# Hashed attention feeding a gated MLP: pair loads moved into the first layers and behind marks, earlier preparation of pairs, a new start

## The chip, the core and the metric

One core of a Trainium2 chip. The metric is the device time of one execution in microseconds (us), median of several. The profile's span is mostly 1.7 to 2.5 us shorter than the time of the same execution (once 3.5), because the time also holds what lies around the program's own instructions. A run over 1.5% above the fastest of its kernel is slow; all ratios are of fast runs, and where a kernel had slow runs, the time given here is the median of its fast ones.

## The reference, cut to what matters

```python
q_bits = (einsum('bhsd,dk->bhsk', q, proj) > 0)     # 6 hash bits per token
k_bits = (einsum('bhsd,dk->bhsk', k, proj) > 0)
mask   = q_bucket[:, :, :, None] == k_bucket[:, :, None, :]
scores = where(mask, scale * q @ k.T, -1e9)
attn   = softmax(scores)                            # B, H, S, D = 4, 8, 768, 64
x      = (attn @ v) as [B*S, H*D]                   # 3072 x 512
h      = x @ w_in;  g = h * cos(h);  out = g @ w_out  # d_ff 2048
```

Four batches of eight heads. Two heads make a pair (16 pairs, numbered 0 to 15). A head is six units; a unit is one score (two matmuls), one exponential on ScalarE over 128x768 and one value step (six matmuls). There are 192 units, 0 to 191; unit u holds the exponential number u + 1.

## The kernel before

The mask comes for free: six hash bits, scaled, are appended as rows to Q and K, so that only equal buckets survive the exponential. Preparing a pair takes: a load (three DMAs of 384 KB), casts to fp16 on GpSimd, 32x32 block transposes on VectorE, the hash on TensorE, and the transposition of Q and K. From pair 5 on the transposition is a DMA, started by SyncE; it brings Q and K in one piece, and VectorE then copies K's rows to their own tile. The bit rows go in by four small DMAs.

```python
    def load(pr, eng):                       # three DMAs; nat has three buffers
        ...
            eng.dma_start(out=t_, in_=heads_ap(src, pr))
    def dma_transposes(pr, hh):              # SyncE's queue
        nc.sync.dma_start_transpose(out=qx(pr)[...], in_=n16_rows(pr)[...])
    def k_copy(pr, hh):                      # VectorE: waits for that DMA
        nc.vector.tensor_copy(out=kx(pr)[0:D, hh, :], in_=qx(pr)[D:P, hh, :])
    def norm(h):                             # VectorE: the division of a head (cut)
        ...                                  # dv, tot, rc, and last:
            nc.vector.tensor_tensor(out=dst, in0=tot[:, :, 0:D], in1=rc..., op=ALU.mult)   # xn
    def xtrans(b, ft):                       # SyncE's queue again
        nc.sync.dma_start_transpose(out=xT[(b, ft)], in_=xn[(b, ft)]...)
    ...
        for n in range(1, NP):
            s0 = 12 * (n - 1) - (0 if n < NEARLY else 4 if n == NEARLY else 6)
            ...
            elif NEARLY + 1 < n < NP - 1:
                at(s0 - 1, lambda n=n: load(n + 1, nc.gpsimd))
            ...
                at(s0, start)                # casts, block transposes, cast of V
                at(s0 + 2, hsh)              # two DMA transposes
                at(s0 + (5 if n == NEARLY else 3), hsh2)   # hash
                at(s0 + 7, kc)               # K copies, bit rows
```

The first layer of the MLP (L1) of a batch stands in one block, TensorE alone, after unit 55, 103 and 151; the second layer is spread over the units of the next batch. L1 reads `xT`, so it needs the last division of its batch. VectorE, GpSimd and SyncE take their work in program order, as their timelines below show.

The softmax here doesn't subtract the row's maximum and nothing guards it: scores larger than these inputs give would overflow.

## Time and profile before

| | before |
|---|---|
| time, median (range) | 310.13 us (309.94 to 310.41) |
| span of the profiled run | 308.4 us |
| first exponential starts | 9.26 |
| 56th starts (last ahead of the first L1) | 58.91 |
| 104th (last ahead of the second L1) | 125.04 |
| 192nd (the last) | 254.75 |

The page's part on the chain that ended last says which engine's work the end can be followed back through:

```profile
PE 89%; ACT 6%; DVE 3%; issue 1%; ACTq 0%; DVEq 0%
```

### The profile page before, as it was taken

How to read it: one execution, taken by the hardware profiler on the slowest of the kernel's cores; microseconds unless marked ns; L12 is line 12 of the kernel's file. 1: busy time of each engine (PE TensorE's matmuls, PEld its weight loads, DVE VectorE, ACT ScalarE, POOL GpSimd, SP SyncE). 2: the span in 40 equal slices, each digit the busy share in tenths (PEclk: the TensorE clock that was granted, in tenths of full speed). 3: DMA queues.
4: the chain of work that ended last, by engine and by line, in shares of the span. 5: the costliest groups of instructions: out<-in, count | busy, mean ns of one | idle time of the engine just before them, and what ended most of it. 6: DMA issues, size and time to landing. Idle time of an engine off the chain costs nothing.

```text
span 308.4 us, 7711 instructions
## 1 busy us (share of the span) xinstructions
PE 300.1 (97%) x3090; PEld 182.8 (59%) x3090; DVE 201.8 (65%) x434; ACT 234.3 (76%) x288; POOL 109.4 (35%) x180
## 2 busy tenths in 40 slices
PE   8899999899999999999999999999999999999995
PEld 3577677556566666555566666555566664565444
DVE  3665466877598988866777878766777343577211
ACT  3788999977899999766899999766899993577000
POOL 4898258378384684400064584100030000000000
PEclk9999999999999999999999999999999999999998
DMA  6969969289469856700169979200133223100121
GB/s 205 376 109 163 333 86 214 33 140 192 163 172 268 215 162 168 217 2 0 45 80 234 234 146 199 48 18 2 53 62 89 68 62 94 36 0 0 62 76 69
DMA packets 45332, 37.74 MB, mean 122 GB/s; under 512 B 32264, under 2 KB 39200, under 8 KB 45296
## 3 DMA queue, kind: packets, MB, share of 16 engines
q1 hardware_dynamic: 38080, 19.35, 28.9%
q0 software_dynamic: 6576, 17.17, 21.0%
q10 hardware_dynamic: 640, 0.72, 0.7%
q8 instruction: 24, 0.39, 0.5%
q14 instruction: 12, 0.10, 0.1%
HBM read 27.26 MB, written 6.29 MB: 109 GB/s over the span
## 4 chain that ended last, share of the span: by engine, by line
PE 89%; ACT 6%; DVE 3%; issue 1%; ACTq 0%; DVEq 0%
PE m_ps L370 26%; PE s_ps L320 18%; PE s_ps L252 18%; PE av_ps L278 10%; PE m_ps L320 6%; ACT pt L258 5%; PE m_ps L164 4%; PE av_ps L320 2%; PE s_ps L408 1%; PE m_ps L354 1%; PE m_ps L224 1%; DVE g L337 1%; DVE blkq L151 1%; ACT cos L332 1%; PE av_ps L164 1%
## 5 line engine op out<-in xcount | busy, mean ns | idle before, releaser
L258 ACT ACTIVATE pt<-s_ps,exp_bias 128x768 f16<-128x768 f32 x192 | 161.7, 899 | 11.1 <-PE s_ps L252 9.7
L370 PE MATMUL m_ps<-wout,g 128*128 128x512 f16 x368 | 105.6, 379 | 0.1
L252 PE MATMUL s_ps<-qx,kx 128*128 128x512 f16 (+1 forms) x384 | 93.8, 326 | 2.6 <-ACT pt L258 1.2
L278 PEld LDWEIGHTS <-pt 128*128 128x128 f16 x1152 | 58.7, 97 | 21.7
L320 PEld LDWEIGHTS <-win 128*128 128x128 f16 x512 | 50.0, 98 | 34.6 <-issue 0.2
L278 PE MATMUL av_ps<-vx,pt 128*128 128x65 f16 x1152 | 65.7, 193 | 0.0
L320 PE MATMUL s_ps<-xT,win 128*128 128x384 f16 x352 | 62.3, 326 | 0.1
L337 DVE TENSOR_TENSOR g<-s_ps,cos 128x768 f16<-128x768 f32 x44 | 42.1, 958 | 28.1 <-ACT cos L332 28.1
L332 ACT ACTIVATE cos<-s_ps,cos_bias 128x768 f16<-128x768 f32 x44 | 39.7, 901 | 26.8 <-PE s_ps L320 25.4
L252 PEld LDWEIGHTS <-kx 128*128 128x128 f16 x384 | 35.2, 97 | 31.1 <-issue 3.3
L138 POOL CAST vx<-natv 128x768 f16<-128x768 f32 x16 | 13.3, 829 | 92.8 <-PE av_ps L278 87.8
L370 PEld LDWEIGHTS <-g 128*128 128x128 f16 x368 | 31.2, 98 | 20.1 <-issue 3.3
L376 DVE COPY ob<-m_ps 128x512 f32<-128x512 f32 x23 | 15.8, 686 | 22.6 <-PE m_ps L370 22.6
L320 PE MATMUL m_ps<-xT,win 128*128 128x384 f16 x120 | 27.6, 326 | 0.0
L332 ACT ACTIVATE cos<-m_ps,cos_bias 128x384 f16<-128x384 f32 x30 | 16.3, 578 | 7.0 <-PE m_ps L320 7.0
L305 DVE TENSOR_TENSOR xn<-tot,rc 128x384 f16<-128x384 f32 x24 | 20.1, 839 | 0.8
L337 DVE TENSOR_TENSOR g<-m_ps,cos 128x384 f16<-128x384 f32 x30 | 15.7, 550 | 1.3 <-ACT cos L332 1.0
L300 DVE COPY dv<-av_ps 128x65 f32<-128x65 f32 x24 | 5.1, 211 | 16.9 <-PE av_ps L278 16.9
L140 POOL TENSOR_TENSOR vhalf<-natv 128x384 f32<-128x384 f32 x16 | 15.9, 996 | 0.0
L133 POOL CAST n16x<-natq 128x768 f16<-128x768 f32 (+1 forms) x16 | 13.1, 822 | 5.1 <-DMA natq<-in_q_dram 5.1
L133 POOL CAST n16x<-natk 128x768 f16<-128x768 f32 (+1 forms) x16 | 13.0, 813 | 5.5 <-DMA natk<-in_k_dram 5.5
L151 DVE STREAM_TRANSPOSE blkq<-natq 128x768 f32<-128x768 f32 x15 | 14.6, 975 | 0.3
(77 smaller groups left out, 274.8 us busy)
## 6 DMA issues: line engine op xcount, KB each, us to landing
out_dram<-ob SPq DMA_DIRECT2D x23, 256.0 KB
natq<-in_q_dram POOLq DMA_DIRECT2D x11, 384.0 KB, 3.9
natk<-in_k_dram POOLq DMA_DIRECT2D x11, 384.0 KB, 4.7
natv<-in_v_dram POOLq DMA_DIRECT2D x11, 384.0 KB, 5.7
win<-in_moe_w_in_dram POOLq DMA_DIRECT2D x4, 512.0 KB, 7.3
wout<-in_moe_w_out_dram POOLq DMA_DIRECT2D x16, 128.0 KB, 5.1
natq<-in_q_dram SPq DMA_DIRECT2D x4, 384.0 KB
natk<-in_k_dram SPq DMA_DIRECT2D x4, 384.0 KB
```

The costliest lines, as they stand in the source:

```text
L133: engs[w].tensor_copy(out=o_, in_=i_)
L140: nc.gpsimd.tensor_tensor(out=half, in0=nv[:, :, 0:3, :], in1=nv[:, :, 3:6, :], op=ALU.add)
L151: nc.vector.transpose(out=blk[pr][w].rearrange("p h t c r -> p (h t c r)"), in_=nat[pr][w].rearrange("p h f -> p (h f)"))
L252: nc.tensor.matmul(out=sp[:, c, 0:c1 - c0], lhsT=kx(pr)[:, hh, jt * P:(jt + 1) * P], rhs=qx(pr)[:, hh, c0:c1], start=True, stop=True)
L258: nc.scalar.activation(out=pt, in_=sp.rearrange("p c n -> p (c n)")[:, 0:S], func=ACTF.Exp, bias=exp_bias, scale=EXP_SCALE)
L278: nc.tensor.matmul(out=bank[:, qt * W:qt * W + D + 1], lhsT=pt[:, qt * P:(qt + 1) * P], rhs=vx_bufs[pr % 3][:, hh, jt, 0:D + 1], start=Fal ...
L305: nc.vector.tensor_tensor(out=dst, in0=tot[:, :, 0:D], in1=rc.unsqueeze(2).to_broadcast([P, T, D]), op=ALU.mult)
L320: nc.tensor.matmul(out=halves[c][:, 0:C2], lhsT=win_t[ft][:, ff * P:(ff + 1) * P], rhs=xT[(b, ft)][:, 3 * c:3 * c + 3, :], start=(ft == 0) ...
L332: nc.scalar.activation(out=c_, in_=h_, func=ACTF.Sin, bias=cos_bias, scale=1.0)
L337: nc.vector.tensor_tensor(out=g_, in0=h_, in1=c_, op=ALU.mult)
L370: nc.tensor.matmul(out=o_ps, lhsT=g[:, qt * P:(qt + 1) * P], rhs=wout_t[ff], start=(ff == 0), stop=(ff == NFF - 1))
L376: nc.vector.tensor_copy(out=ob, in_=o_ps)
```

## The change

The intent: a smoother first attention batch (work at half units, fixed lists of heavy units), a shorter start, and the big loads out of the attention batches into the L1 blocks, where they are meant to disturb nobody. "Mark" means a tiny copy on GpSimd that reads a unit's weights, so that the load behind it is not issued sooner. `OFF` gives the units of casts, transposes, hash, and K copies with their bit rows; `LATE` gives them outright for single pairs.

```diff
+    SECOND = [0.5, 1.5, 3.5, 4.0]
+    PREP = {1: [0.5, 2, 4.5, 6, ...], 2: [...], 3: [...], 4: [...]}
+    LATE = {5: [44, 46, 49, 51], 6: [54, 56, 57, 61], 7: [66, 68, 69, 73],
+            10: [101, None, 105, 107], 14: [149, None, 153, 155]}
+    OFF = (-8, -6, -4, -1)
+    LOADS = {9: 58, 10: 87, 13: 111, 14: 135}
+    IN_L1 = {0: {8: 7, 12: 8}, 1: {3: 11, 9: 12}, 2: {3: 15}}
+    T_L1 = {10: (1, 1), 14: (2, 1)}
...
-        nc.scalar.dma_start(out=proj2, in_=proj.rearrange("(c p) i -> p c i", c=2))
+        for b_, eng in enumerate((nc.scalar, nc.sync, nc.scalar, nc.sync)):
+            eng.dma_start(out=projblk[32 * b_:32 * b_ + 32, :, b_, 0:NBITS], in_=proj...)
...
-            elif NEARLY + 1 < n < NP - 1:
-                at(s0 - 1, lambda n=n: load(n + 1, nc.gpsimd))
+            if n in LOADS:
+                def late_load(n=n):
+                    nc.gpsimd.tensor_copy(out=mark, in_=pts[divmod(LOADS[n], T)][:, 0:1])
+                    load(n, nc.gpsimd)
+                at(LOADS[n], late_load)
...
-                at(s0, start)
-                at(s0 + 2, hsh)
-                at(s0 + (5 if n == NEARLY else 3), hsh2)
-                at(s0 + 7, kc)
+                steps = [start, hsh, hsh2, kc]
+                units = LATE.get(n, [s0 + d_ for d_ in OFF])     # s0 is now 12 * (n - 1)
```

In the same reckoning the old offsets were -6, -4, -3, +1. So everything moves one or two units earlier, and the K copies move from +1 to -1.

More of the change, by code (lines that the diff above doesn't have):

```diff
@@ L56 @@
     COOL = False
+    SECOND = [0.5, 1.5, 3.5, 4.0]
+    PREP = {1: [0.5, 2, 4.5, 6, 7.5, 9, 9.5, 12, 14], 2: [14.5, 12, 12, 16, 18, 21, 22.0, 23.0, 24.5], 3: [22.5, 22, 24, 26, 28, 29.5, 32, 34, 34.5], 4: [36, 33, 34, 37, 39, 40, 44, 45.0, 46]}
+    LATE = {5: [44, 46, 49, 51], 6: [54, 56, 57, 61], 7: [66, 68, 69, 73], 10: [101, None, 105, 107], 14: [149, None, 153, 155]}
+    WIN = [6, 14, 22, 30]
+    LAG = 2
+    OFF = (-8, -6, -4, -1)
+    LOADS = {9: 58, 10: 87, 13: 111, 14: 135}
+    IN_L1 = {0: {8: 7, 12: 8}, 1: {3: 11, 9: 12}, 2: {3: 15}}
+    T_L1 = {10: (1, 1), 14: (2, 1)}
+    MAXP = 3
+    EXTRA = {49}
+    HEAVY = set(int(x) for n in PREP for x in PREP[n][3:]) | set(int(x) for x in SECOND) | EXTRA
     glob = ctx.enter_context(tc.tile_pool(name="glob", bufs=1))
@@ L80 @@
     warm = glob.tile([P, 1], FP32, name="warm")
-    wz = glob.tile([P, 512], FP16, name="wz")
-    proj2 = glob.tile([32, 2, NBITS], FP32, name="proj2")
     projblk = glob.tile([P, 2, 4, 8], FP32, name="projblk")
@@ L144, in cast_v, with blocks @@
             out=vs_bufs[pr % 3][:, :, 0:D], in0=two, in1=half[:, :, 2, :], op=ALU.add)
-    def blocks(pr, hh=None):
+    def blocks(pr, hh=None, ws=(0, 1)):
         if pr not in blk:
             blk[pr] = [blkp.tile([P, 2, T, 2, 32], FP32, name=nm) for nm in ("blkq", "blkk")]
-        for w in range(2):
+        for w in ws:
             if hh is None:
@@ L408, in warmup @@
             nc.tensor.matmul(
-                out=s_ps[1][:, 1, :], lhsT=wz[:, 0:P], rhs=wz, start=True, stop=True,
-                skip_group_check=True)
+                out=s_ps[1][:, 1, :],
+                lhsT=nc.const_aps.tensor(1.0, [P, P], BF16),
+                rhs=nc.const_aps.tensor(1.0, [P, 512], BF16),
+                start=True, stop=True, skip_group_check=True)
     with tc.manual_schedule():
@@ L415 @@
         aps = [heads_ap(src, 0) for src in (q, k, v)]
-        nc.scalar.dma_start(out=proj2, in_=proj.rearrange("(c p) i -> p c i", c=2))
         nc.sync.dma_start(out=nat[0][0][:, 0], in_=aps[0][:, 0])
         nc.scalar.dma_start(out=nat[0][1][:, 0], in_=aps[1][:, 0])
+        nc.vector.memset(exp_bias, EXP_BIAS)
+        nc.vector.memset(projblk, 0.0)
+        for b_, eng in enumerate((nc.scalar, nc.sync, nc.scalar, nc.sync)):
+            eng.dma_start(
+                out=projblk[32 * b_:32 * b_ + 32, :, b_, 0:NBITS],
+                in_=proj.rearrange("(c p) i -> p c i", c=2))
         nc.sync.dma_start(out=nat[0][0][:, 1], in_=aps[0][:, 1])
@@ L423 @@
         load(2, nc.sync)
-        nc.vector.memset(wz, 0.0)
-        nc.vector.memset(exp_bias, EXP_BIAS)
         nc.vector.memset(cos_bias, math.pi / 2.0)
-        nc.vector.memset(projblk, 0.0)
         nc.vector.memset(bitrow, 2.0 * BIT)
@@ L441 @@
         warmup(8)
-        for b_ in range(4):
-            nc.vector.tensor_copy(
-                out=projblk[32 * b_:32 * b_ + 32, :, b_, 0:NBITS], in_=proj2)
-        blocks(0, 0)
+        blocks(0, 0, (0,))
+        blocks(0, 0, (1,))
         cast_qk(0, 0, (nc.scalar, nc.scalar))
@@ L457 @@
         warmup(1)
-        rows_copy(nc.vector, pe_transposes(0, 0, 1, av_ps[0]))
+        rows_copy(nc.vector, pe_transposes(0, 0, 1, av_ps[0], range(0, 1)))
         rows_copy(nc.scalar, pe_transposes(0, 0, 0, m_ps[0], range(0, 3)))
         rows_copy(nc.vector, pe_transposes(0, 0, 0, m_ps[1], range(3, 6)))
+        rows_copy(nc.vector, pe_transposes(0, 0, 1, s_ps[1][:, 0, :], range(1, 6)))
         blocks(0, 1)
@@ L472, with casts, hash_a @@
         L1_AT = {UB * b + 7: b - 1 for b in range(1, B)}
-        acts = {}
+        acts, in_l1 = {}, {}
         def at(u, f):
             acts.setdefault(u, []).append(f)
-        at(0, second_a)
-        at(1, second_b)
+        at(SECOND[0], second_a)
+        at(SECOND[1], second_b)
         for w_ in range(2):
-            at(2 + w_, lambda w_=w_: rows_copy(nc.vector, pe_transposes(0, 1, w_, m_ps[w_])))
+            at(SECOND[2 + w_], lambda w_=w_: rows_copy(nc.vector, pe_transposes(0, 1, w_, m_ps[w_])))
+        def casts(n):
+            cast_qk(n, None, (nc.gpsimd, nc.gpsimd))
+            cast_v(n)
         for n in range(1, NP):
-            s0 = 12 * (n - 1) - (0 if n < NEARLY else 4 if n == NEARLY else 6)
-            def start(n=n):
-                cast_qk(n, None, (nc.gpsimd, nc.gpsimd))
-                blocks(n)
-                cast_v(n)
+            s0 = 12 * (n - 1)
             if n < NEARLY:
                 at(s0 + 2, lambda n=n: load(n + 2, nc.sync if n + 2 < NEARLY else nc.gpsimd))
-            elif NEARLY + 1 < n < NP - 1:
-                at(s0 - 1, lambda n=n: load(n + 1, nc.gpsimd))
+            if n in LOADS:
[3 more added lines that the diff above has]
+                at(LOADS[n], late_load)
             if n < NEARLY:
-                o_ = 3 if n == 1 else 0
                 held = {}
-                def hash_a(half, n=n, held=held):
-                    ts = range(3 * half, 3 * half + 3)
-                    held["bh"] = hash_sums(
-                        n, m_ps[half], [(j % 2, j // 2, ts) for j in range(4)],
-                        held.get("bh"), 3 * half)
+                def hash_a(n=n, held=held):
+                    held["bh"] = hash_sums(n, m_ps[1], [(j % 2, j // 2, range(T)) for j in range(4)])
                 def hash_b(n=n, held=held):
@@ L503, in trp, with start @@
                     rows_copy(nc.vector, pe_transposes(n, hh, w, m_ps[1 - w]))
-                at(s0 + o_, start)
-                for half in range(2):
-                    at(s0 + 3 + o_ + half, lambda hash_a=hash_a, half=half: hash_a(half))
-                at(s0 + 5 + o_, hash_b)
-                for i in range(4):
-                    at(s0 + (6 if n == 1 else 7) + o_ + i, lambda trp=trp, i=i: trp(i // 2, i % 2))
-            else:
+                steps = [lambda n=n: casts(n), lambda n=n: blocks(n, 0), lambda n=n: blocks(n, 1)]
+                steps += [hash_a, hash_b]
+                steps += [lambda f=trp, i=i: f(i // 2, i % 2) for i in range(4)]
+                units = PREP[n]
+            else:
+                def start(n=n):
+                    cast_qk(n, None, (nc.gpsimd, nc.gpsimd))
+                    blocks(n)
+                    cast_v(n)
                 def hsh(n=n):
@@ L519, in kc @@
                     bits_dma(n, (0, 1, 2, 3))
-                at(s0, start)
-                at(s0 + 2, hsh)
-                at(s0 + (5 if n == NEARLY else 3), hsh2)
-                at(s0 + 7, kc)
+                steps = [start, hsh, hsh2, kc]
+                units = LATE.get(n, [s0 + d_ for d_ in OFF])
+            for u_, f in zip(units, steps):
+                if u_ is None:
+                    in_l1[T_L1[n]] = f
+                else:
+                    at(u_, f)
         for i in range(4):
-            at(6 + 8 * i, lambda i=i: weights_in(i))
-        done = 0
+            at(WIN[i], lambda i=i: weights_in(i))
         for u in range(U):
@@ L531 @@
             pend.append((h, jt))
-            for _ in range(2):
-                if len(pend) > (4 if u < T else 2):
-                    av_step()
+            for f in acts.get(u - 0.5, ()):
+                f()
+            if u >= 54:
+                avs = min(2, len(pend) - 2)
+            elif u in HEAVY:
+                avs = len(pend) - MAXP
+            else:
+                avs = min(2, len(pend) - (4 if u < T else LAG))
+            for _ in range(avs):
+                av_step()
             for f in acts.get(u, ()):
@@ L557 @@
                             weights_out(2 * ff + 1)
-                        elif ff == NFF // 2:
-                            load(NEARLY + 2, nc.gpsimd)
+                    if (bb, ff) in in_l1:
+                        in_l1[(bb, ff)]()
+                    if ff in IN_L1[bb]:
+                        if bb > 0:
+                            nc.gpsimd.tensor_copy(out=mark, in_=g_tiles[(bb, ff - 1)][:, 0, 0:1])
+                        load(IN_L1[bb][ff], nc.gpsimd)
                     if ff in AVS[bb > 0] and len(pend) > 0:
```

## The prediction

> **What bounds the kernel now.** I read the page first (engine shares, slices), then the stretches by stage, then ScalarE's and TensorE's lines in order of time, and last GpSimd's at the start. The page's first part:
>
> ```profile
> span 308.4 us, 7711 instructions
> PE 300.1 (97%) x3090; PEld 182.8 (59%) x3090; DVE 201.8 (65%) x434; ACT 234.3 (76%) x288; POOL 109.4 (35%) x180
> ...
> PE   8899999899999999999999999999999999999995
> ```
>
> By this TensorE has nothing to give. But the records of pipelined matmuls overlap, so a full row does not mean that TensorE sets the pace. Cut into the first attention batch (8.70 to 59.10), the first block of first layers (L1, 59.10 to 82.50) and the second batch (82.50 to 125.30):
>
> ```profile
> 8.70:59.10 50.40, 47.97 (x834) 34.38 (x835) 32.88 (x74) 45.96 (x56) 34.76 (x50) 1.00 0.85 194
> 59.10:82.50 23.40, 23.27 (x151) 13.93 (x151) 16.84 (x26) 18.47 (x24) 13.42 (x35) 1.00 0.81 159
> 82.50:125.30 42.80, 42.80 (x514) 26.38 (x513) 36.10 (x89) 40.04 (x49) 28.54 (x40) 1.00 0.72 188
> ```
>
> The first number after the stretch is its length; then follow PE, PEld, DVE, ACT and POOL. Both attention batches do some 48 to 56 exponentials, yet the first, which has no second layer to do beside them, takes 50.4 us against 42.8. So the first batch is where time could lie. There the exponentials come in runs, with gaps between them:
>
> ```profile
> 25.91 10.19 ACT L258 ACTIVATE pt<-s_ps,exp_bias 128x768 f16<-128x768 f32 x12 [0.18 <-PE s_ps L252]
> 36.60 10.17 ACT L258 ACTIVATE pt<-s_ps,exp_bias 128x768 f16<-128x768 f32 x12 [0.50 <-PE s_ps L252]
> 46.95 7.58 ACT L258 ACTIVATE pt<-s_ps,exp_bias 128x768 f16<-128x768 f32 x9 [0.18 <-PE s_ps L252]
> 54.98 4.86 ACT L258 ACTIVATE pt<-s_ps,exp_bias 128x768 f16<-128x768 f32 x6 [0.45 <-PE s_ps L252]
> ```
>
> The last run gives the floor: (4.86 - 0.90) / 5 = 0.79 us from one to the next. From the first, which starts at 9.26, to the 56th, at 54.98 + 5 x 0.79 = 58.94, are 55 steps: 49.7 us where the floor is 43.5. Some 6.2 us is all that any reordering of this batch can win. What makes a step longer is seen on TensorE:
>
> ```profile
> 34.60 0.50 PE L252 MATMUL s_ps<-qx,kx 128*128 128x512 f16 x2
> 34.94 0.34 PE L278 MATMUL av_ps<-vx,pt 128*128 128x65 f16 x6
> 35.21 0.27 PE L164 MATMUL m_ps<-blkq,projblk 128*32 128x96 f32 x1
> ...
> 35.68 0.50 PE L252 MATMUL s_ps<-qx,kx 128*128 128x512 f16 x2
> ...
> 39.40 0.49 PE L252 MATMUL s_ps<-qx,kx 128*128 128x512 f16 x2
> 39.72 0.34 PE L278 MATMUL av_ps<-vx,pt 128*128 128x65 f16 x6
> 39.90 0.50 PE L224 MATMUL m_ps<-ident,n16x 128*128 128x128 f16 x6
> 40.24 0.49 PE L252 MATMUL s_ps<-qx,kx 128*128 128x512 f16 x2
> ```
>
> The starts give the price of each piece: a score 0.33, a value step 0.18, six transposes 0.34; half a hash makes a unit of 35.68 - 34.60 = 1.08. With two score buffers, the next score cannot start before an exponential ends (0.90), and its exponential starts some 0.59 after it; twice the floor is 1.58, so there is next to no slack. A unit costs the larger of 0.79 and the sum of its pieces, and a short unit hardly repays a long one.
>
> In the second batch the unit is 0.33 + 0.18 + 1.5 x 0.216 (second layer) = 0.83; that is TensorE's own work and stays.
>
> **What the Trainium skill says.** "Perfetto Trace Analysis", section Identifying the Most-Contended Engine: matmul busy share is no measure of headroom. The trace agrees: 48.0 of 50.4 us busy in a stage that could be some 6 us shorter. "ScalarE: Activation LUTs", section What ACT_TABLE_LOAD costs: an ACTIVATE with a pointer bias takes 280 ns + 0.833 per column and overlaps the next by 93 ns. For 768 columns that is an estimate of 920 long, 827 apart; the trace has 901 and 790, and I use these. "DMA: Bandwidth & Descriptors", section Issuing engines are not separate DMA queues: all queues share 16 engines. The trace bears this out at the start: the values of pair 0, on their own queue, are used only from 9.42.
>
> **The change, part by part.**
>
> Start. The ones for warming up no longer wait for a memset, the projection goes straight to its block form (four copies, 0.70 us on VectorE, go), and the first half of K is issued 0.46 us earlier (first on its queue rather than second). The hash of the first half waits for K's block transpose, now done at about 4.65 instead of 5.05: 0.4 won. Only one sixth of K is transposed ahead of the first score: the 0.56 us copy before Q's copy becomes some 0.2: another 0.4. First score: 8.72 - 0.8 = 7.9.
>
> Then a catch. The first value step is now in unit 3, not 4 (the list of heavy units forces it). It needs the sums of V:
>
> ```profile
> 9.42 0.83 POOL L138 CAST vx<-natv 128x768 f16<-128x768 f32 x1 [1.38 <-DMA natv<-in_v_dram]
> 10.22 0.99 POOL L140 TENSOR_TENSOR vhalf<-natv 128x384 f32<-128x384 f32 x1
> 11.29 0.46 POOL L142 TENSOR_TENSOR vtwo<-vhalf 128x128 f32<-128x128 f32 x1
> 11.83 0.46 POOL L143 TENSOR_TENSOR vs<-vtwo,vhalf 128x128 f16<-128x128 f32 x1
> ...
> 12.73 0.33 PE L267 MATMUL av_ps<-vs,delta_w 128*128 128x390 f16 x1
> ```
>
> They are ready at 12.29, and nothing makes V land sooner (issued 0.4 later, with less ahead of it). With scores of units 1, 2, 3 at 8.3, 9.8 and 10.5, TensorE would stand at unit 3 from 10.85 to about 12.3. Score 4 would come at 12.6 or 12.7; it was 12.41. So the 0.8 is given back.
>
> Units 4 to 55. Before: from exponential 4 (13.03, three 0.79 steps after the one at 10.66 counted as unit 1) to 58.94 are 45.9 us for 51 steps, floor 40.3: excess 5.6. After, with a full hash at 0.85 (before, the step to the run at 54.98 is 54.98 - 53.63 = 1.35 = 0.33 + 0.18 + 0.85; the chain has 0.79 for its 16 matmuls alone), counting each unit in the order of the changed program:
>
> - a hash with no value step, 0.33 + 0.85 = 1.18, costs 0.39: pairs 2, 3, 4, 5, so 1.56; pair 1's has two value steps, 1.54, and a block transpose that is late by a quarter: 1.0.
> - transposes with no value step, 0.67: free. With one, 0.85: 0.06, four times; with two (the half-unit marks), 1.02: 0.23, five times; with one and the opening 0.17 of a head: 0.23. Sum 1.6.
> - the two transposes in unit 4, 1.18: 0.4; a token step with two value steps, 1.2: 0.4; two value steps with an opening, 0.86: 0.07, four times, 0.3.
>
> In all 5.3, against 5.6: 0.3 won. A further 0.3 may go too: the step before the run at 36.60 is 36.60 - (25.91 + 10.19 - 0.90) = 1.40, of which that unit's work accounts for only 1.08.
>
> The loads. Pairs 7, 8, 11, 12 and 15 go into the L1 blocks, 9, 10, 13, 14 behind marks; transposes and hashes move one or two units earlier. From 59 on the chain of waits is TensorE almost alone, and the gaps on POOL (35% busy) and the DMA queues are on nobody's path. The marks add seven small copies to POOL: nothing. Hashes in even units instead of odd: same sum. I put 0 on all of it.
>
> Sum: 0.8 won at the start, 0.8 to 1.0 given back at the value sums, 0.3 to 0.6 won in the batch: 0.3 to 0.6, or with early V 1.3 more, so between 309.8 and 308.3.
>
> **Rivals.** First: the value sums come sooner, or the wait is shorter than I think, and all of the start counts: 308.3. For it: V's queue is less crowded; against: 9.42 is a landing of the slowest of 16 engines. Second: the smoothing works better than my sum, because a light unit does repay a heavy one (in the second batch steps alternate above and below 0.83): then up to half of the 5.3 goes, and the time is 306. Against it: twelve units before take 10.2 to 10.7 with the same mix, which only a no-slack count gives. Third: a late load or a mark in POOL's queue holds up a later cast, and TensorE waits in a batch: 311 to 313. Against: each pair is loaded ten units or more ahead of its use, and I find none whose buffer is still held.
>
> **Range and chances.** I lean to a mean of these, 308.8. The whole excess, 6.2, is what 2% asks for, so faster by over 2% would need nearly all of it: 4%. Slower by over 2% needs a new wait of 6 us in stages that have none: 2%. The range is 306.6 to 310.6.
>
> **What would show it.** First exponential near 8.4 (was 9.26); TensorE waiting for GpSimd's sums just before the first opening matmul, until about 12.3; the 56th exponential at 57.5 to 58.7; the second batch 42.8 within 0.3; L1 blocks 23.4. Wrong, if the 56th comes before 57 (slack), if the second and third batch change by over 0.5 (loads matter), or if TensorE shows waits on casts.

## More of the kernel before

One line of the list of waits will matter later; it reads: engine, tile, its line, what it waited for, us in all, times, longest.

```profile
DVE kx L243 <- DMA qx<-n16x: 0.7, 2, 0.4
```

VectorE's K copies hardly ever wait for the DMA transpose that feeds them.

## The result, and the profile after

The changed kernel took 314.86 us (fast runs 314.09, 314.86, 314.94; one slow run, 319.58) against 310.08 in the same rounds (four runs, of which the table above has three): a ratio of 1.0145 (1.0124 to 1.0166). A ratio is the mean time of one kernel's fast runs over that of the other's of the same rounds, so not quite the ratio of the medians quoted. It is slower by 1.5%, outside the predicted range. The granted clock is no rival: it was 1.000 over the profiled run, and 0.997 over that of before.

The page of the changed kernel: span, busy shares, TensorE's slices, and the engines of the chain that ended last.

```profile
span 312.2 us, 7600 instructions
PE 300.5 (96%) x3025; PEld 181.1 (58%) x3026; DVE 201.0 (64%) x434; ACT 233.1 (75%) x288; POOL 110.6 (35%) x187
...
PE   6999999999999999799999999999999999999995
...
PE 68%; ACT 10%; DVE 8%; DMA 7%; issue 2%; POOL 2%; ACTq 0%; DVEq 0%; POOLq 0%
```

The busy shares say next to nothing (97 to 96% for TensorE). The chain says a lot: 7% of the end now goes through DMAs and 8% through VectorE. The time is found by setting the starts of the same exponential side by side (worked out from the two traces):

| exponential | before | after | difference |
|---|---|---|---|
| 1st | 9.26 | 9.63 | +0.37 |
| 56th | 58.91 | 57.99 | -0.92 |
| 70th | 93.95 | 93.02 | -0.93 |
| 71st | 95.56 | 95.79 | +0.23 |
| 104th | 125.04 | 125.38 | +0.34 |
| 105th (second L1 lies before it) | 151.80 | 154.09 | +2.29 |
| 131st | 175.63 | 178.99 | +3.36 |
| 153rd (third L1 lies before it) | 220.92 | 225.02 | +4.10 |
| 192nd | 254.75 | 258.99 | +4.24 |

So the first batch does win; then time is lost in four places: 1.15 at unit 70, 1.95 at the second L1, 0.9 at unit 129, 0.8 at the third L1. They sum to 4.8, nearly all of the way from -0.92 to +4.24, which is 5.2.

**The start.** First the wait list, then engines in order of time (start, us, engine, line, what):

```profile
PE av_ps L174 <- DMA projblk<-in_proj_dram: 1.1, 1, 1.1
```

```profile
7.74 0.84 PE L234 MATMUL m_ps<-ident,n16x 128*128 128x128 f16 x6
...
11.17 0.46 POOL L153 TENSOR_TENSOR vs<-vtwo,vhalf 128x128 f16<-128x128 f32 x1
...
12.13 0.33 PE L277 MATMUL av_ps<-vs,delta_w 128*128 128x390 f16 x1
```

TensorE stands 1.1 us for the projection's four small DMAs, and the six transposes take 0.84 where before's took 0.50. The sums of V, feared in the prediction, are ready at 11.63 (before: 12.29).

**The second L1.** Two of the waits over the whole run, then the chain that leads to L1's first matmul, then VectorE and SyncE there, before and after:

```profile
DVE kx L253 <- DMA qx<-n16x: 7.2, 7, 1.6
...
PE s_ps L330 <- DMA xT<-xn: 2.5, 2, 1.8
```

```profile
117.41 4.90 DMA qx<-n16x
...
122.33 0.89 DVE kx L253
...
124.22 0.56 DVE xn L315
...
125.20 3.20 DMA xT<-xn
...
128.44 0.48 PE s_ps L330 x2
```

```profile
121.24 1.15 DVE L305 TENSOR_TENSOR xn<-tot,rc 128x384 f16<-128x384 f32 x1
122.41 1.24 SPq L311 DMA_TRANSPOSE xT<-xn  x1
122.41 1.03 DVE L243 COPY kx<-qx 64x768 f16<-64x768 f16 x2
...
123.75 0.72 SPq L217 DMA_DIRECT2D qx<-br  x1
```

```profile
121.68 0.46 DVE L253 COPY kx<-qx 64x768 f16<-64x768 f16 x1 [1.65 <-DMA qx<-n16x]
...
124.22 0.56 DVE L315 TENSOR_TENSOR xn<-tot,rc 128x384 f16<-128x384 f32 x1
124.44 0.67 SPq L227 DMA_DIRECT2D kx<-br  x1
...
125.20 2.06 SPq L321 DMA_TRANSPOSE xT<-xn  x1
```

The K copies' 0.7 us of waiting has become 7.2. VectorE stands at a K copy for a DMA transpose that takes 4.9 us; behind it in program order stand the division and, on SyncE, the `xT` transpose that L1 waits for. A small part is SyncE's own queue: the bit rows now stand ahead of `xT` there, so `xT` starts 0.4 us after the division's end (124.78) and not at once, as it did before. In the trace the transpose that the K copies wait for has packets of a pair load in flight beside it (192 and 101 packets for the two transposes of that pair); with none in flight, the same transposes take 2.0 to 2.1 us in this kernel, but for one of 2.5. Before, the one of the same pair took 3.0 and nobody minded: the K copies came after the division.

**Unit 70.** VectorE and GpSimd in order of time, before and then after:

```profile
88.19 1.00 POOL L140 TENSOR_TENSOR vhalf<-natv 128x384 f32<-128x384 f32 x1
...
88.45 1.14 DVE L305 TENSOR_TENSOR xn<-tot,rc 128x384 f16<-128x384 f32 x1
```

```profile
87.28 0.84 POOL L143 CAST n16x<-natq 128x768 f16<-128x768 f32 x1
...
87.53 2.54 DVE L315 TENSOR_TENSOR xn<-tot,rc 128x384 f16<-128x384 f32 x1
...
88.83 0.82 POOL L148 CAST vx<-natv 128x768 f16<-128x768 f32 x1
89.63 1.29 POOL L150 TENSOR_TENSOR vhalf<-natv 128x384 f32<-128x384 f32 x1
90.10 1.57 DVE L253 COPY kx<-qx 64x768 f16<-64x768 f16 x2
```

The division's last step (`xn`) takes 0.56 us alone. Before, it took 1.14 beside `vhalf`; here it takes 2.54, through a run of three casts. Those casts stand just there because on GpSimd they come behind the load of pair 9, and GpSimd waits 3.1 us at its mark, until the weights of unit 58 are there. Before, a load stood ahead of these casts too, but none was held so long, and they began at 84.93. What follows on VectorE is late, the block transposes of pair 7 too, and its hash waits.

### The profile page after: what moved, and what is told of

Its sections match the earlier page's. It is cut to its first block, busy times and chain, and to the rows that moved or that the text cites. A ratio compares the mean times of both kernels' runs of the same rounds, so it can differ in the third digit from the quotient of the medians.

```text
span 312.2 us, 7600 instructions
## 1 busy us (share of the span) xinstructions
PE 300.5 (96%) x3025; PEld 181.1 (58%) x3026; DVE 201.0 (64%) x434; ACT 233.1 (75%) x288; POOL 110.6 (35%) x187
## 4 chain that ended last, share of the span: by engine, by line
PE 68%; ACT 10%; DVE 8%; DMA 7%; issue 2%; POOL 2%; ACTq 0%; DVEq 0%; POOLq 0%
PE m_ps L380 19%; PE s_ps L330 17%; PE s_ps L262 11%; ACT pt L268 9%; PE m_ps L330 6%; PE av_ps L288 6%; DMA qx<-n16x 4%; PE m_ps L174 3%; PE av_ps L330 2%; DVE kx L253 2%; DMA xT<-xn 2%; DVE xn L315 1%; DMA projblk<-in_proj_dram 1%; PE m_ps L364 1%; PE m_ps L234 1%
## 5 line engine op out<-in xcount | busy, mean ns | idle before, releaser
L288 PEld LDWEIGHTS <-pt 128*128 128x128 f16 x1152 | 56.9, 97 | 19.5
L288 PE MATMUL av_ps<-vx,pt 128*128 128x65 f16 x1152 | 63.8, 193 | 0.0
L150 POOL TENSOR_TENSOR vhalf<-natv 128x384 f32<-128x384 f32 x16 | 17.6, 1098 | 0.0
L253 DVE COPY kx<-qx 64x768 f16<-64x768 f16 x22 | 12.1, 576 | 7.4 <-DMA qx<-n16x 7.2
L506 POOL COPY mark<-pt 128x1 f16<-128x1 f16 x4 | 0.8, 188 | 40.0 <-ACT pt L268 40.0
```

The source lines that it names most:

```text
L150: nc.gpsimd.tensor_tensor(out=half, in0=nv[:, :, 0:3, :], in1=nv[:, :, 3:6, :], op=ALU.add)
L288: nc.tensor.matmul(out=bank[:, qt * W:qt * W + D + 1], lhsT=pt[:, qt * P:(qt + 1) * P], rhs=vx_bufs[pr % 3][:, hh, jt, 0:D + 1], start=Fal ...
```

## The experiments

Three theories for the late part. A puts the loss down to the marks and loads in new places, B to the earlier preparation, above all the K copies; a third adds that loads in flight slow the DMA transposes. Losses by place below are differences from before in the trace; each time is given against before's of the same chip and rounds.

### Which half of the change?

**First half alone**: the new start and first batch, late pairs as before.

```diff
-    LATE = {..., 10: [101, None, 105, 107], 14: [149, None, 153, 155]}
-    OFF = (-8, -6, -4, -1)
+    OFF = (-6, -4, -3, 1)
-    LOADS, IN_L1: new places, with marks
+    LOADS, IN_L1: the old places (8 at 65, 9 at 77, ... 15 at 149), no marks
```

> The changed kernel with its late part put back as it was (loads without marks at the old units, old offsets of the late pairs); the new start and the new first batch stay. If everything lost is lost after the first batch, the 56th exponential starts near 58.0 us as in the changed kernel and each later one is 0.92 us earlier than before: 309.2 us. If the new first batch itself sets up a later wait (for example at the 71st exponential, 1.15 us late in the changed kernel, although pairs 5, 6 and 7 have the same units in both), 310 to 311.

310.69 against 310.31, ratio 1.000 (0.9957 to 1.0043). No loss, but no gain either (the second of the two cases in the text): the profiled run is 1.55 ahead at the 56th exponential and loses 0.75 at unit 96 and 0.4 near unit 124. The weights of a score (PEld is TensorE's weight load) now wait for the bit rows of K, longest 1.0 us; before, that wait was 0.2 in all:

```profile
PEld L262 <- DMA kx<-br: 1.3, 2, 1.0
```

An earlier first batch runs into a preparation that is not earlier.

**Second half alone**, on the kernel before.

```diff
+    LATE, OFF, LOADS, IN_L1, T_L1 and the marks of the change; start and first batch as before
```

> The converse of the first experiment: the kernel before, with its own start and first batch, and only the late part of the change (loads in the L1 blocks and behind marks, earlier units, transposes of pairs 10 and 14 inside L1). If the late part is the whole loss, 310.1 plus the 5.2 us counted at the 71st, 105th, 130th and 153rd exponential and the small ones: 315 to 316. If first batch and late part act together, 311 to 313 or over 317.

317.63 against 309.97, ratio 1.022 (1.0158 to 1.0282). The loss comes with this half. In its profile it is 1.16 at unit 70, 1.2 at the second L1, 2.0 at unit 129 and 4.3 at the third L1: the places are the same, the sizes are not fixed. The time lies over the 315 to 316 foreseen for a loss that is this half's alone, and just over the 317 that the text took for a sign of both halves acting together; but the runs go from 313.78 to 318.19 and the interval overlaps that of the change, so this stays undecided.

### Marks, or early preparation?

**Loads at the old places without marks, early preparation kept.**

```diff
-    LOADS = {9: 58, 10: 87, 13: 111, 14: 135};  IN_L1 = {0: {8: 7, 12: 8}, 1: {3: 11, 9: 12}, 2: {3: 15}}
+    LOADS = {8: 65, 9: 77, 10: 89, 11: 101, 12: 113, 13: 125, 14: 137, 15: 149}; IN_L1 = {0: {8: 7}, 1: {}, 2: {}}
-                    nc.gpsimd.tensor_copy(out=mark, ...)
```

> The changed kernel with the loads of pairs 8 to 15 at the old units and without marks; the earlier units of casts, transposes, hashes and K copies of the late pairs stay. Theory A (the marks hold GpSimd up, its casts come late, so the transposes by DMA come late, and the K copies then stand in VectorE's order ahead of the division and the transpose of the attention output): the losses go, 309 to 310, and the L1 blocks start with no wait for xT. Theory B (moving the K copies two units earlier is bad by itself): 313 to 315, with the wait for xT at the second and third L1 block still there. Theory C (loads under way slow the DMA transposes): the old places also have loads under way near the transposes, so 312 to 315.

323.30 against 310.31, ratio 1.0399 (fast runs 321.23 and 325.36, and two slow ones). Worse by far, and outside all three forecasts: 7.2 us at the second L1, though nothing at unit 70. So the marks and new places are not what costs the time at the L1 blocks; without them it costs more.

**No marks, loads otherwise as changed.**

```diff
-                    nc.gpsimd.tensor_copy(out=mark, in_=pts[...])
-                        if bb > 0: nc.gpsimd.tensor_copy(out=mark, in_=g_tiles[...])
```

> The changed kernel without the seven small copies that hold the late loads back; program order of the loads stays, so GpSimd issues them as soon as it comes to them and goes on with its casts. Theory A: casts early, DMA transposes early, no wait for xT, 71st exponential on time: 309 to 310. Theory B: the K copies are as early in VectorE's order, so 312 to 315. Theory C: loads earlier and apart from the transposes, 309 to 311.

313.05, ratio 1.0083 (1.003 to 1.0136). The losses move (1.0 at unit 93, 1.7 at 141, 1.9 at the third L1, none at 70 or at the second L1): a mark decides which transposes a load meets, not whether it meets any. At unit 70, though, the mark is what counts: there is no loss in any run without marks (the first half alone, the old places, this one), and 1.14 to 1.16 wherever the load of pair 9 stands behind its mark at 58 and nothing else holds the casts. So the first half of theory A (marks hold GpSimd up) is right at that one place.

**Old offsets, new loads and marks.**

```diff
-    OFF = (-8, -6, -4, -1)
+    OFF = (-6, -4, -3, 1)      # and the entries of pairs 10 and 14 in LATE taken out
```

> The changed kernel with the old units of casts, transposes, hashes and K copies for pairs 8 to 15; the loads stay in the L1 blocks and behind marks. Theory A: the casts still come late, but the K copies stand behind the division again, so the waits for xT (1.8 and 0.8 us) go and the 1.15 us at the 71st exponential stays: 310 to 311. Theory B: the same, 310 to 311. Theory C: the transposes are still slowed, 312 to 315.

310.49, ratio 0.9992 (0.995 to 1.0035). No wait for `xT` and none of the K copies for their transposes is left; the 1.14 at unit 70 stays, and 0.5 at unit 96.

**Only the K copies back to +1**, and with them their bit rows; all else of the change kept.

```diff
-    OFF = (-8, -6, -4, -1)
+    OFF = (-8, -6, -4, 1)
```

> The changed kernel with one thing put back: the K copies and bit rows of pairs 8, 9, 11, 12, 13 and 15 two units later, as before (pairs 10 and 14 stay). If the K copy ahead of the division in VectorE's order is what makes the late DMA transposes felt, the waits at the 105th, 130th and 153rd exponential (1.95, 0.85 and 0.82 us) go and 1.15 us at the 71st stays: 310 to 311. If the slowed transposes act by another way (casts, hashes, SyncE's queue), these waits stay at 1 us or more each: 313 to 315.

311.09 against 310.24, ratio 1.002 (0.998 to 1.0061). This one number takes away the waits at both L1 blocks (1.95 and 0.8 us), and some 0.7 of the 0.9 at unit 129. The 1.15 at unit 70 stays, and unit 96 now loses 0.75.

**Only the K copies early**, with their bit rows, on the kernel of the first half alone.

```diff
-    OFF = (-6, -4, -3, 1)
+    OFF = (-6, -4, -3, -1)
```

> The converse: the new first batch with the whole old late part, and only the K copies of pairs 8 to 15 two units earlier. Old loads are under way beside most DMA transposes (2.5 to 5.1 us from issue to last packet in the kernel before). If the early K copy is enough, VectorE stands at the K copies in most pairs and the L1 blocks wait for xT: 313 to 325. If it needs the earlier casts or the marks too, 309.5 to 311.

319.21, ratio 1.0304 (1.0242 to 1.0365). It loses 6.2 at the second L1 and 4.1 at units 141 and 142. From its list of waits:

```profile
DVE kx L253 <- DMA qx<-n16x: 20.6, 12, 6.7
...
PE s_ps L330 <- DMA xT<-xn: 4.9, 2, 4.5
```

The pair of runs settles it: K copies and bit rows ahead of the division are enough to cause the loss at L1, and taking them back is enough to cure it. The two were always moved together. The trace of the change gives the bit rows 0.4 us of the delay; no run moves one alone.

**Pairs 10 and 14 not transposed inside L1.**

```diff
-    LATE = {..., 10: [101, None, 105, 107], 14: [149, None, 153, 155]}
+    LATE = {...}               # pairs 10 and 14 by OFF
```

> The changed kernel with the transposes of pairs 10 and 14 back at a unit of their own (102 and 150) instead of inside L1. If this part of the change does nothing for good or ill, 314 to 315.5 with the same waits. If it adds to SyncE's queue ahead of the L1 blocks and makes the wait for xT longer, over 316; if the in-L1 transposes were a cause, under 313.

314.75 against 309.97, ratio 1.0186 (1.0128 to 1.0244), one slow run left out: no better than the change itself, which had 1.0145. That part is not the cause.

### Keep the early K copies, move the loads away

If the K copies hurt only because a load slows their transposes, it should be enough to keep loads and transposes apart.

**Each late load behind its pair of transposes.**

```diff
-    LOADS = {9: 58, 10: 87, 13: 111, 14: 135}
+    LOADS = {9: 71, 10: 82, 13: 106, 14: 130}
```

> The changed kernel with the four marked loads at other units: 9 at 71 rather than 58, 10 at 82 rather than 87, 13 at 106 rather than 111, 14 at 130 rather than 135, so that each lands before the next pair's DMA transposes. If the collision of these loads with the transposes is the first cause, each transpose takes 2.0 to 2.5 us from issue to last packet, VectorE does not wait at the K copies, the four losses go and the gain of the first batch stays: 308.5 to 309.5. If early K copies are bad even with free transposes, 312 or more.

311.13, ratio 1.0025 (0.9993 to 1.0057), over the 308.5 to 309.5 hoped for. Nearly all transposes take 2.0 to 2.1 us, the waits for `xT` are gone with the K copies still early, and so is the loss at unit 70. A new loss of 1.8 comes at unit 93: the two K copies of pair 8, 0.36 us each when alone, take 3.76 together while GpSimd issues the load of pair 10 and does the casts behind it; what holds them was not tested.

**Only the load of pair 9 moved.**

```diff
-    LOADS = {9: 58, ...}
+    LOADS = {9: 71, ...}
```

> The changed kernel with the load of pair 9 alone moved from unit 58 to 71, behind the casts of pair 7. If the 1.15 us at the 71st exponential come from GpSimd doing that load before pair 7's casts, which then run beside VectorE's division (2.54 us instead of 1.14), this one loss goes and the others stay: 312.7 to 314. If not, no change, 314 to 315.

313.26, ratio 1.0133 (1.0058 to 1.0207); fast runs 312.68, 313.26 and 317.2, too far apart to tell the two forecasts from each other. The kernel is still slower than before, so this load alone does not cure it. What holds the division at unit 70 is settled by the run with a mark ahead of the casts of pair 7, below.

**Three loads in the second L1** (and in the first), two of the four loads behind units left.

```diff
-    LOADS = {9: 58, 10: 87, 13: 111, 14: 135}
-    IN_L1 = {0: {8: 7, 12: 8}, 1: {3: 11, 9: 12}, 2: {3: 15}}
+    LOADS = {10: 71, 14: 119}
+    IN_L1 = {0: {8: 7, 11: 8, 14: 9}, 1: {3: 11, 7: 12, 11: 13}, 2: {3: 15}}
```

> A better placing, if the cause is right: the changed kernel with the loads of pairs 9 and 13 moved into the L1 blocks too (where no transposes run) and those of 10 and 14 right behind units 71 and 119, before the next pair's casts. All DMA transposes of q and k free (2.0 to 2.5 us), no VectorE wait at the K copies over 0.5, no wait for xT, no loss at the 71st exponential: the gain at the 56th stays to the end: 308.3 to 309.5. If early K copies or the earlier units cost by themselves, 311 or more.

311.45 against 309.97, ratio 1.0044 (1.0019 to 1.0068). Better than the change, yet not the gain foreseen (308.3 to 309.5). In the trace it is 2.0 us ahead of before up to unit 75, still 1.9 at unit 80, and loses 2.1 at unit 81; after that nothing over 0.2. The long step at 81 goes back to one division of 3.19 us (97.44 to 100.63), beside GpSimd's casts of pair 8 (97.85 to 100.22), which had waited behind the load at 71.

**The same with a longer warm-up.**

```diff
-        warmup(8)
+        warmup(10)
```

> The same with ten instead of eight opening matmuls. In the changed kernel the matmuls of the first hash took 0.34 to 0.37 us each in five profiles (first exponential at 9.5 to 10.0) and 0.24 to 0.27 in four others (8.5 to 8.8): TensorE stood from 4.35 until the projection landed at 5.2. If the pause lets the clock fall back, two more matmuls keep it up: first exponential at 8.8 or less, 0.5 to 1 us faster than the kernel it is compared with. If the landing of the projection alone sets it, no change.

310.67, ratio 1.0024 (1.0009 to 1.0039). The 3.19 us division is there again, to the digit. The four runs' spans lie within 0.7 us (308.7 to 309.4), against 1.9 without it. What the longer warm-up gives can't be read from this pair: the run without it had a quick start too (first exponential at 8.74, here 8.89).

### What holds the division: casts, or the load?

**Marks two units earlier.**

```diff
-    LOADS = {10: 71, 14: 119}
+    LOADS = {10: 69, 14: 117}
```

> As the kernel with three loads in the second L1, but the marks of pairs 10 and 14 at units 69 and 117 in place of 71 and 119. There the division of a head (head 11, asked for at 97.44) took 3.19 us on VectorE, until 0.4 us after GpSimd's three back-to-back casts (97.85 to 100.22), and TensorE lost 2.1 us at unit 81. Theory (a division stands until GpSimd's run of casts is over): the load is issued 1.6 us earlier, so the casts end near 98.7 and the division takes some 1.6; the loss at unit 81 falls to about 0.5 and the profiled span to about 306.9 (306.4 to 307.6). Rival (the long division is due to the load's packets in flight, or to its issue): the load is still in flight at 97.4 and its issue ends 1.6 us earlier, so the first rival expects a division of 3 us and a loss of 2 again, span 308.4; the second expects 0.56 and no loss.

309.67 against 310.29, ratio 0.9983 (0.9964 to 1.0003), one slow run left out. VectorE and GpSimd at that place:

```profile
98.09 1.60 DVE L315 TENSOR_TENSOR xn<-tot,rc 128x384 f16<-128x384 f32 x1
98.26 1.00 POOL L150 TENSOR_TENSOR vhalf<-natv 128x384 f32<-128x384 f32 x1
```

The division takes 1.60, as the casts' theory said, though the load is in flight. But the loss at unit 81 stayed (2.2), against that theory's 0.5: the load, issued earlier, now met the second DMA transpose of pair 7, which took 7.4 us, and the K copy waited for it (waits between 94 and 105 us):

```profile
DVE kx L253 <- DMA qx<-n16x: 2.4, 1, 2.4
```

A right mechanism and a wrong sum: the second one took over.

**One mark ahead of the casts, load where it was.**

```diff
     LOADS = {10: 71, 14: 119}
+    CAST_MARK = {8: 74}
...
+                at(CAST_MARK[n], lambda n=n: nc.gpsimd.tensor_copy(out=mark, in_=pts[...][:, 0:1]))
```

> As the kernel with three loads in the second L1, loads and marks where they are there; one more tiny copy on GpSimd, which reads the weights of unit 74, stands ahead of the casts of pair 8, so that these begin at about 98.1 in place of 97.85 minus nothing else moved, that is after the division has started and ended (97.44 to 98.0). Theory (casts hold the division): the division takes 0.56 us, the loss of 2.1 us at unit 81 is gone, and the profiled span is 306.3 to 307.0 unless the bit rows of pair 8 then come late for unit 96 (0.5 to 0.8 us, as in other runs whose first batch ended early). Rival (the load in flight holds it): division 3 us, loss as before, span 308.4 or more.

310.03 against 310.29, ratio 0.9978 (0.9957 to 1.0000); the profiled span is 307.2.

```profile
98.37 0.56 DVE L316 TENSOR_TENSOR xn<-tot,rc 128x384 f16<-128x384 f32 x1
...
99.03 0.98 POOL L144 CAST n16x<-natq 128x768 f16<-128x768 f32 x1
```

With the load's issue beside it (until 98.78), the division takes 0.56, and the loss at unit 81 is gone. It is the casts. The time is still that of before within the noise.

This is what the Trainium skill's page "SBUF — State Buffer", section Who interferes with whom, states: a VectorE instruction with two inputs in SBUF contends with a GpSimd instruction that reads SBUF, and the loser blocks. The traces agree, and add a number: the loser is not let in between two casts that follow each other closely. In the long cases `xn` ends 0.41 to 0.43 us after the end of the last GpSimd instruction that held it. That is the third cast with three loads in the second L1 (100.22 + 0.41) and after the change (89.65 + 0.42), and `vhalf` in the run with earlier marks (99.26 + 0.43). In the first two, `vhalf` had begun by then and took 1.31 and 1.29 in place of 1.00: there GpSimd was the one held up.

**The same mark in the changed kernel**, ahead of the casts of pair 7.

```diff
     LOADS = {9: 58, 10: 87, 13: 111, 14: 135}
+    CAST_MARK = {7: 62}
```

> The changed kernel with one tiny copy more on GpSimd, which reads the weights of unit 62 and stands ahead of the casts of pair 7; the load of pair 9 behind unit 58 stays where it is. Theory (the run of casts held the division): the division near 87.5 takes 0.56 to 1.2 us in place of 2.54, the loss of 1.15 us at unit 70 is gone or under 0.3, and the losses at units 104, 129 and 152 stay, 1.8, 0.9 and 0.8; span 311.0 to 311.5, time about 313.5. Rival (the load in flight): the loss at 70 stays.

Ratio 1.0076 (1.0043 to 1.0109) from two fast runs, 311.37 and 313.89; two more were slow. The division takes 0.56 and the loss at unit 70 is gone. But the second L1 now loses 4.0 in the profiled run, not 1.95: waits that hang on DMA collisions do not stay put when the batch arrives 1.8 us sooner.

### The start

TensorE's six transposes ahead of the first score took 0.84 to 0.85 us in seven of the fourteen profiles with the new start and eight warming matmuls, and 0.49 to 0.50 in the other seven, in no relation to what was changed later. The Trainium skill's page "TensorE: Matmul & The Clock Gate", Part 1, says that the array is slow until it has been busy for a window of about 3.4 us and that the window runs free, so that the same kernel can differ between runs. That fits the split: the packed trace records when the full clock was first granted, at 4.3 to 5.1 us in the seven quick profiles and at 8.7 to 10.2 in the seven slow ones. In all of them TensorE is busy from 0.78 to 4.35 and then idle for 0.67 to 1.40 us. The length of that pause does not decide it: 0.67 went with a slow start, 1.10 with both.

**Longer warm-up and the cast mark.**

```diff
     CAST_MARK = {8: 74}
-        warmup(8)
+        warmup(10)
```

> The kernel with three loads in the second L1 and the extra mark before the casts of pair 8, with ten warming matmuls in place of eight, so that they reach to about 5.2, where the projection lands, with no idle time of TensorE between. In that kernel's own profile TensorE was cold at the start (hash matmuls 0.37, six transposes 0.84, first exponential at 9.66) and the span was 307.2. Theory (an idle TensorE before the hash decides whether the six transposes at 7.5 run at 0.50 or 0.84): first exponential at 8.9, no later loss, span 306.2 to 306.8, time 308.0 to 308.8, and the runs lie within 0.6 us of each other. Rival (the start's gain is swallowed later, by the bit rows for unit 96): span 307.2, time as before or 0.3 under.

308.67 against 310.32, ratio 0.9953 (0.9942 to 0.9965), five of six runs within 0.25 us (308.57 to 308.80; the sixth 309.43). TensorE's start:

```profile
0.78 4.42 PE L419 MATMUL s_ps<-const-bfloat16-1.0 128*128 128x512 bf16 x10 [0.78 <-PEq L627]
...
7.13 0.49 PE L235 MATMUL m_ps<-ident,n16x 128*128 128x128 f16 x6
```

First exponential at 8.62, 1.78 ahead at the 56th, 1.04 ahead at the last. The time is the one foreseen (308.0 to 308.8), the spread (0.86) a little over the 0.6. This kernel beats both. That the longer warm-up is the reason is not shown: two profiles with ten matmuls, both quick, against seven of fourteen with eight are too few, and the next run does without it.

**The old way of loading the projection, eight warming matmuls.**

```diff
-        four DMAs straight into projblk
+        nc.scalar.dma_start(out=proj2, ...)      # first on its queue
+        four copies projblk <- proj2 on VectorE
```

> The same kernel with eight warming matmuls, but with the projection loaded and copied as in the kernel before (one small load first on its queue, four copies on VectorE) in place of four loads straight into block form. Theory (the four loads land at 5.2, later than the copies would be done): the hash starts near 4.7 as before in place of 5.3 to 5.4, the first exponential comes at 8.6 to 9.0, span 306.2 to 306.8. Rival (the block form's loads win time, as the change intends): the hash starts no earlier than 5.3, first exponential 9.3 or later, span 307 or more.

308.78, ratio 0.9946 (0.9933 to 0.9958), runs from 308.25 to 310.02. The hash does start at 4.46, but it then waits at 5.16 for K's block transpose, the six transposes take 0.85 (the full clock is first granted at 10.13, though the pause before the hash is only 0.11 us), and the first exponential comes at 9.59: that step of the theory fell in the profiled run. Its time is as good as the last one's; the profiled run is the slowest of the five. The two can't be told apart.

## Why the prediction was wrong

- **The step that failed** is "The loads": "I put 0 on all of it". It measured +5.2 from the 56th exponential to the last. The text names the earlier transposes and hashes, but not the K copies, which move with them and cross the division: that is what costs the 1.95 and 0.8 us at the L1 blocks. The mark and load of pair 9, also put at nothing, cost the 1.15 at unit 70. The 0 was argued from the chain of waits and GpSimd's 35% busy share. Both describe the program as it stood before. Moving the K copies across the division gave VectorE's queue a new order, in which a DMA's duration lies on the path to L1; the 0.7 us of waiting before was no measure of that.
- The argument "each pair is loaded ten units or more ahead of its use" looked only at when a load must land. What counted is what it meets on the way: transposes of 2.0 us become 2.8 to 4.9, and casts that come due behind it fall on a division.
- **Rival three**, a late load holding a cast up (311 to 313), came nearest and was too small. Its form was different too: at unit 70 the casts were not late for their own pair, they held up VectorE; at the L1 blocks it was no cast that counted, but a DMA transpose.
- **The start**: 0.8 won was predicted, 0.37 was lost in the profiled run. The hash was put at 4.65 and started at 5.46, because the four projection DMAs land that late; I had looked at K's block transpose alone. The clock took the rest: 0.84 for six transposes in place of 0.50. In the seven quick profiles with eight warming matmuls the first exponential came at 8.38 to 8.77, so there 0.5 to 0.9 was won, about as predicted (near 8.4). What the text lacked is that the start comes in two forms.
- **The catch** at the value sums (until 12.3) decided nothing in the profiled run: the sums were ready at 11.63 and the value step ran at 12.13. In the quick starts it came true, smaller than foreseen: TensorE stands 0.4 to 0.8 us for the sums in five of the seven. The longest (in the run without transposes inside L1):

```profile
11.70 0.33 PE L277 MATMUL av_ps<-vs,delta_w 128*128 128x390 f16 x1 [0.84 <-POOL vs L153]
```

- **The first batch** was right: 57.5 to 58.7 predicted for the 56th exponential, 57.99 measured. But it came about differently: a start 0.37 later and 1.29 won from the first exponential to the 56th, where I had 0.8 to 1.0 given back and 0.3 to 0.6 won. That the 56th fell in the range is luck: two misses of opposite sign. In the quick starts the same first batch had its 56th at 56.8 to 57.5, at the lower end or under it.
- **Two smaller slips**: from its own terms the sum is 0.1 to 0.6 won, not 0.3 to 0.6. And a sentence cut from the text called V's queue its own: V goes on ScalarE's queue, behind the projection and half of K, so its use from 9.42 shows nothing about shared DMA engines. What does agree with them is the second L1: a load issued by GpSimd stretches a transpose issued by SyncE from 2.0 to 4.9 us.
- The test named in advance, "if the second and third batch change by over 0.5 (loads matter)", was the right one: the table of exponentials answered it at once. From the 56th exponential to the 104th it went from -0.92 to +0.34, 1.26 longer: loads and preparation do matter.

What stays open: the size of single losses, which shifts by several us with small shifts in time (1.2 to 7.2 at the second L1); why GpSimd's next cast gets ahead of a waiting VectorE; what K copies and bit rows cost one without the other; and the 1.6 us that the profiled run with the old projection lost between units 84 and 93.

## What to carry to other kernels

An early step that waits for a DMA, put ahead of other work on an engine that works in order, turns that DMA's worst duration into a wait of everything behind it; before moving it, look at what stands next in that queue and at what the DMA will share its time with. A wait of zero in the profile tells how late the wait was asked for, not how quick the thing is. And when a gain of one stage does not reach the end, set the starts of the same instruction side by side over the whole run: here four jumps told more than all the busy shares.

## What the Trainium skill lacked or had wrong

- "SBUF — State Buffer", Who interferes with whom: whoever issues first is said to have the shared ports for the whole instruction (this of VectorE's two-port modes), and the other to block. What happens at the end of that instruction is not said. Here VectorE stayed blocked over three GpSimd casts that followed each other closely: 0.56 us alone became 2.54 and 3.19.
- "DMA: Bandwidth & Descriptors", DMA Transpose (X-bar): no figure for a transpose beside other transfers. Here an SBUF to SBUF transpose of 128 x 768 took mostly 2.0 to 2.1 us from issue to last packet with no load in flight (single ones up to 3.7), 2.8 to 4.9 beside a pair load in the changed kernel, 7.4 with the marks two units earlier, and up to 10.2 with the loads at the old places.
- "TensorE: Matmul & The Clock Gate", Part 1: what it says fits. It has no figure for how a warm-up of 3.57 us, a little over its window, ends: seven of fourteen profiles were slow, whatever the pause behind it, and one more (with the old projection) was slow with a pause of 0.11 us. With ten warming matmuls the transposes were quick in both profiles, which are too few to tell.
